# Maxima of q as a row of the transposed q from unit 2 on, and the last two tiles of a unit projected as 64-row pairs, in a fused attention and maxout kernel

## The chip, the cores and the metric

The kernel runs on one core of a Trainium2 chip. The core has five engines with instruction streams of their own: TensorE (PE: matmuls, with the weight load PEld beside it), VectorE (DVE), ScalarE (ACT), GpSimd (POOL) and SyncE (SP, which here only issues transfers). They share an on-chip memory (SBUF) and eight PSUM banks, into which PE writes its products. The metric is the time of one execution on the device in microseconds; lower is better. Three executions of the kernel before took 292.72, 292.85 and 293.96 us; the median is 292.85.

## The reference

Two stages that follow each other. The first is attention in linear form with a feature map, the second a feed-forward layer whose three hidden projections are joined by a maximum:

```python
def phi(x):                                    # x: 8 batches, 8 heads, 576 rows, 64 columns
    proj = np.einsum('bhsd,df->bhsf', x, w_phi)                      # 64 -> 128
    proj = proj - np.max(np.abs(proj), axis=-1, keepdims=True)
    return np.concatenate([np.exp(proj), np.exp(-proj)], axis=-1)
q_p, k_p = (phi(q), phi(k))
kv = np.einsum('bhsf,bhsd->bhfd', k_p, v)
z = np.sum(k_p, axis=2)
num = np.einsum('bhsf,bhfd->bhsd', q_p, kv)
den = np.einsum('bhsf,bhf->bhs', q_p, z)[..., None] + 1e-06
attn = num / den
x = attn.transpose(0, 2, 1, 3).reshape(8 * 576, 512)
h = np.maximum(np.maximum(x @ w1, x @ w2), x @ w3)                   # 512 -> 768
out = h @ w_out                                                      # 768 -> 512
```

All inputs and the output are float32. The row maximum of |proj| is what the change is about: for q it is subtracted from proj before the exponents are taken.

## The kernel before

**Units.** The 64 pairs of batch and head are handled four at a time: 16 units, each with 18 tiles of 128 rows (two pairs of heads, 8 full tiles each, and tiles 8 and 17, which hold the last 64 rows of each head). The tiles of a unit are worked in five groups, L37: four groups of four tiles and one of two, `(8, 2)`, the two last tiles.

**One unit, step by step.** q and k come in. For units 0 to 3 (BY_PE) POOL's queue loads them and turns float32 into bf16 on the way, and PE transposes them (L491), after which DVE copies them into qkT (L494). From unit 4 on SP loads them as float32, POOL casts them (L477), and SP transposes them by DMA (L506). SP loads v. In qkT, rows 0 to 63 hold the transposed q, rows 64 to 127 the transposed k.

- Projections G: for a group of four tiles PE makes a pair of 64-row products for each tile, q into the bank psq and k into the bank psk (L533). For the group of two tiles it makes one full product of 128 rows and 256 columns for each tile, and q and k lie side by side in the bank psq (L528).
- DVE takes the maxima of |proj| from these banks (L552): of q into mqp, of k into mk. ACT takes the two exponents of k into Ek (L546).
- From mk ACT makes the factors em (L584), and POOL multiplies v by them into vab (L588; units 0 and 1 in halves of nine tiles, one of them by DVE), and em itself is copied beside it (L598).
- Maxima of q, first form (`by_product`, units 0 to 3, since SUBT is 4): PE makes q's projection again, now transposed, into the bank psm (L615), and then for each tile of the group adds a product of the maxima with a negative identity (L618): 18 such products in a unit.
- Maxima of q, second form (units 4 to 15): PE transposes the maxima into the bank pmT (L560, the node R), ACT or DVE copies them to mT (L564), and a DMA writes mT as row 64 of qkT (L568, the node V), over k's first row. From units 4 on SP issues it; ACT issues it for units below V_ACT, which is 4, so so far for none. Then one matmul for a group, with a weight matrix wphi_m whose row 64 is -1 (L613), gives the projection less the maximum. Since the row replaces k's data, V waits for all of the unit's projections.
- ACT takes the two exponents of q from psm into Eq (L626).
- K: 72 products of Ek and vab (L642), copied to kv (L647). N: 40 products of Eq and kv (L660), divided on DVE (L666, L667) into x_sb. For units 0 to 5 PE transposes x_sb (L680), for the others a DMA does (L690), into xT.

**The second stage** runs in chunks of 512 tokens, one for each batch as soon as both of its units are through, and a last one for the 64-row tails of all batches: hidden products (L713), maxima (L719, L721, L723), output products (L741, L746), copies (L754) and stores (L761, by SP). The weights w1, w2, w3 and w_out are loaded by POOL's queue (L421). The maximum of three is taken as x@w1 + max(0, x@(w2-w1), x@(w3-w1)): POOL or DVE subtracts w1 from the two others in place (L788), and the straight part x@w1@w_out is a product (L741) with pm = w1@w_out, which PE makes once (L814) from w1 as it has turned it (L800).

**The order.** Nothing is scheduled at run time. Each step is a node with a number, a kind, costs, dependencies and buffers. The table PLAN, L97 to L243, lists all nodes in order; a word such as `64T10@11.8` says: node 64 on PE (T; D is DVE, A ACT, G POOL, S SP), buffer slots 1 and 0, planned start 11.8. The function plan (L250) reads it, and each engine executes its instructions in the order of the table. The table also fixes which of the eight banks each product gets, and two engines may not read one bank at the same time (locks): they follow one another. A change in the number of nodes or banks needs a new table.

**Fillers.** The function fill (L268) looks at the planned gaps on PE up to 28 us (WARM) and some after, and puts products into them whose result nobody reads (L846, into the bank of the buffer spare).

The queues: SP's loads, stores and transposes are hardware queues; POOL's loads with a change of type (q and k of units 0 to 3, w1, w2, w3, w_out) are a software queue, on which POOL's own engine is busy while it issues (L421 and the q, k loads some 0.7 to 0.9 us each). ACT issues one store at the end (281.41 us).

Of the kernel before, what the change touches and what calls it, by code (L numbers as in the profile page):

```python
# [16 lines left out]
DF = 128  # L17
DM = H * D
DFF = 768
P = 128  # L20
# [22 lines left out]
SUBT = 4  # L43
# [3 lines left out]
JOIN = 2  # L47
MOVE = 5
# [49 lines left out]
2D0@0.5 8S0@0.7 10S@1.3 4S@1.9 0G@0.5 6G0@1.1 7G@1.9 12S0@3.1 3D@0.8 9D@4.5 5D@5.5 11D@6.2 1G@2.8 1051G@3.2 13T1@5.9  # L98
14D0@6.7 82G1@4.0 83G@4.9 17T2@7.5 15T3@7.6 24T004500@8.0 19T67@8.4 18D@7.8 16D@8.3 22D@8.9 27D@9.5 29T12@9.1 39T3@9.3
34T64@10.3 32D@10.1 42D@10.7 37D@11.1 26A@8.6 25A@9.3 31A@9.7 21A@10.2 36A@10.9 35A@11.5 20A@12.0 33D@11.7 38D@12.3  # L100
43D@12.9 28D@13.2 23D@13.8 64T10@11.8 58T6@12.2 65A@12.5 66A@13.0 156G2@5.7 155G@6.6 1061T4@13.0 61T1@13.6 1065T0@14.1
55T5@14.7 52T7@15.2 41A@13.4 60A@13.7 48A0@14.2 62A@14.4 44A@14.9 59A@15.2 40A@15.7 53A@16.0 30A@16.5 57A@17.0
47A0@17.5 63A@17.6 56A@18.1 54A@18.6 49G@14.6 45G@15.7 1054G@16.8 1062D0@14.4 46G@17.6 51G@18.7 50G@19.0 1052G@20.1
84D1@15.6 1066D@15.7 86T4@16.4 90T6@16.9 88T3@17.1 87D1@17.2 89D@17.8 91D@18.4 92T110211@18.0 102T41@18.6 97T35@18.8
112T6@19.1 95D@18.6 96D@19.3 107T70@19.4 103A@19.1 113A@19.6 93A@20.0 108A@20.5 109A@21.1 85S@15.8 105D@19.9 110D@20.5
67T047@21.2 115D@21.1 100D@21.4 106D@22.0 94A@21.6 98A@22.1 104A@22.8 68A@23.3 128T31@22.3 1063T2@22.8 222G0@20.9
159T1@23.4 131T4@24.0 129A@23.7 116D@22.6 69D@23.0 111D@23.3 121A1@24.2 114A@24.4 123G1@24.6 124G@25.7 101D@24.0
137T7@24.6 130A@24.7 139A@25.2 117A@25.6 99A@25.8 138A@26.3 118G@26.0 119G@27.1 122G@28.2 125T0@24.8 132A@26.6
133A@27.3 120A@27.8 134T6@25.3 136A@27.9 135A@28.6 126A@29.0 127A@29.7 223G@29.3 76T30@25.8 1053G@30.2 1057G@31.0
1055G@33.1 1064D@24.6 160D2@25.7 74T2@26.1 70T5@26.5 77D0@26.3 71D1@27.0 75D0@27.6 1071T1@26.8 157D2@28.3 1072D@28.4  # L110
158S@28.5 165T00735400@28.1 161T2@28.7 163T1@29.2 169D@29.0 164D@29.6 168D@29.8 172D@30.4 162D@31.0 166A@30.2
167A@30.8 1073T6@29.3 140T110@30.7 173D@31.6 174T7532@31.9 182D@32.6 1074A@31.3 141A@32.1 181D@33.2 177D@33.8
183T6@32.3 142A@32.5 185A@32.9 180A@33.3 179A@34.0 1069T1@32.7 170A@34.5 1070A@35.0 72T0@34.0 149T31@34.3 178D@34.4
187D@35.0 186D@35.5 188A0@35.5 175A@35.7 191A0@36.2 1067T7@34.6 190G@35.9 189G@38.0 1068A@36.4 1056G@40.1 150D1@35.8
143T2@35.9 80T1@36.2 147T3@36.6 145T7@37.0 144D0@36.5 224D3@37.1 73D1@37.2 146D0@37.8 148D1@38.4 225S@37.3 356S1@38.0
355S0@38.6 359G1@43.2 358G@44.7 201T20@37.4 176A@36.9 184A@37.4 195T5@37.8 192T6@38.3 171A@37.7 81D@39.0 202A@38.2
203A@38.8 290S0@40.3 151T0@38.8 78T4@39.1 153T7@39.4 152D@39.5 1060D@40.2 154D@40.8 79D@41.3 204T3@39.7 226T2@40.0
207T010@40.5 193A@39.3 205A@40.2 206A@40.7 197A@41.0 228T3@41.6 230T7@42.2 227D0@41.7 194A@41.5 196A@42.0 208A@42.5
198T4@42.3 209D@42.3 229D@42.7 232T11625011@42.9 1097T1@43.5 1085T3@44.4 199A@43.1 234A@43.7 231D@43.3 239D@43.7
236D@44.4 212T70@45.3 235D@45.0 233A@45.1 289S1@42.9 293G2@46.7 292G@49.1 1086A1@45.6 200A@46.1 213D0@45.9 360S1@46.0  # L120
1098D@46.5 237A@46.6 1081T5@45.6 250T6@46.5 241T2374@46.7 253D@47.1 244D@47.6 1058D@48.2 248D@48.8 1082A@47.1
247A@47.6 243A@48.1 252A@48.6 238A@48.9 1079T1@47.3 1080A@49.4 251A@49.9 1077T5@48.3 1083T2@49.1 242A@50.2 1078A@50.7
421S0@50.6 1084A@51.2 1089T7@50.0 249D@49.4 254D@50.4 240D@50.7 1090D@51.4 245D@52.0 1059D@52.6 265T11@50.9 262T6@51.4
271T5@51.8 273A@52.3 246A@52.7 272A@53.2 210T0@52.1 214T2@52.4 211D1@53.2 215D0@53.8 1087T7@52.7 1093T3@53.6
216T4@54.5 548S1@51.2 294S2@52.5 422S0@57.8 547S1@58.4 357S0@59.7 266A@53.5 263A@54.0 267A@54.5 268T5@54.8 218T0@55.3
255A1@55.0 264A@55.2 219A@55.8 1099T2@55.6 259T1@56.4 258A1@56.5 257G@55.4 256G@57.5 269A@56.6 260A@57.2 261A@57.8
270A@58.3 1094D@54.7 217D1@55.3 1088D@56.0 1100D@56.7 291S1@61.2 1397G@59.5 361T00364000@56.9 368D@57.7 364D@58.4
1095T7@57.5 1091T2@58.5 1096D@59.0 1092D@59.6 369D@60.2 370T1453@59.3 362A@58.8 375A@60.2 1101T7@59.9 367A@61.0
363A@61.5 379T2@60.9 378D@60.8 377D@61.4 382D@62.0 373D@62.4 381A@62.5 376A@62.9 365D@63.0 383D@63.6 374D@63.9
1102T@61.1 1105T5@62.4 1106T@63.3 384T1@64.6 1103A0@63.3 380A@64.1 274T136@64.6 1107D1@64.8 387A0@64.7 385A0@64.9  # L130
424G0@59.9 366A@65.2 390A0@65.7 550G1@66.5 425G@67.6 295T11721511@66.0 300A@66.7 297A@67.2 388G@68.7 389G@70.8
386S@65.3 275D@66.0 298D@66.7 276D@67.3 281T01@66.5 1109T3@67.0 296A@67.9 372A@68.4 301A@68.9 371A@69.3 283T7@67.9
279T6@68.2 282D0@67.7 284D1@68.4 280D0@69.1 1110T@68.5 1111A2@70.1 299D@69.7 1113T0@69.8 302D@70.3 303D@70.9
304T7642@70.7 305A@71.5 277T3@71.3 307D@71.5 278D1@72.1 311D@72.7 426S0@68.9 484S0@71.8 394T10@71.7 423S2@72.4
396A@72.2 395A@72.8 1114T@71.9 313T5@73.2 1115A3@73.5 220T7@73.4 287T3@73.7 611S0@73.7 610S1@75.2 486S3@76.6 317D@73.7
221D@74.0 308D@74.5 285T1@74.0 286A@74.6 310A@75.3 306A@75.7 288D@75.1 406T040@74.4 391T7@75.5 403T1@75.8 404A@76.2
309A@76.6 405A@77.1 407D@75.7 408D@76.1 312D@77.2 316D@77.8 1125T3@75.9 397T4@76.8 1119T6@77.0 1131T0@77.9 1120D0@78.2
399A@77.4 398A@78.0 392A@78.5 393A@79.2 315A@79.6 318T1@78.8 1132D@79.0 319D1@79.6 321A1@80.0 314A@80.2 324G1@80.4
320S@80.0 551G@80.7 1104S@80.7 411T20@78.8 487G2@81.8 1126A@80.6 1117T4@79.1 1129T6@80.0 1127T0@80.9 400T7@81.8
1118A@81.1 1128A@82.0 322G@82.9 323G@85.0 402A@82.5 401A@83.1 1130D@81.7 412D0@82.3 1139T1@82.0 1140D@83.1  # L140
436T00534600@82.8 1121T0@83.4 442A@83.7 441A@84.3 437A@84.8 438A@85.4 439D@83.7 443D@84.3 444D@84.9 427T2715@84.5
434D@85.5 440D@86.2 430D@86.8 433A@85.9 1122A@86.4 1123T4@85.1 1137T6@86.0 445T1@86.9 325T31@87.1 447A@87.4 326A@87.7
1124A@88.2 1135T0@87.4 1145T2@88.2 327A@88.7 448D@87.9 1138D@88.2 449D@88.8 446A@89.3 450T4@89.1 1133T6@89.2
1136D@89.2 451D0@89.8 331T3@90.0 328T1@90.2 432A@89.7 428A@90.2 429A@90.8 330A@91.3 435D@90.3 1134D@90.9 340T104@90.5
332A@91.8 341A@92.3 342D@91.9 431D@92.2 1149T5@91.6 1150T@92.6 1151D0@94.1 329A@92.7 453A0@93.1 333A@93.4 334T6@93.9
613G0@87.1 335A@94.3 336A@95.0 552S1@82.2 485S1@85.1 553T11407111@94.1 571T3@94.7 614G@88.2 575D@95.2 557D@95.6
560D@96.2 1146T@95.0 454G0@93.5 488G@95.6 574D@96.8 674S0@89.5 675S0@90.1 559A@95.5 558A@96.1 555A@96.6 556D@97.1
561D@97.7 572A@97.3 1108S@90.7 1116S@91.9 337T5@96.3 1141T6@96.4 1152S@94.9 549S1@96.1 1142T@97.3 1147A1@97.6
1143D3@98.8 452S@96.7 562T7421@98.6 573A@98.2 554A@98.6 563A@99.4 339A@99.9 564A@100.2 338A@100.7 569D@99.4 570D@100.1
565D@100.7 1153T3@99.1 1154T@100.1 1155A0@101.7 566D@101.3 576T0@101.4 568A@102.3 567A@102.9 577D1@101.9 415T6@101.5  # L150
413T2@101.8 416D1@102.1 409T5@102.1 347T71@102.4 414D0@102.7 348D1@103.3 1148S@98.4 862S0@99.6 578S@102.2 673S1@102.9
457T40@102.8 469T0@103.0 677G1@96.8 456G@97.9 455G@98.2 459A@103.4 471A@103.9 470A@104.4 349T3@103.1 343T6@103.4
350D0@103.9 344D1@104.6 410D0@105.2 472T021@103.7 466T7@104.9 345T3@105.2 346D1@105.8 460T0@105.5 458A@104.7
579A1@105.2 468A@105.5 467A@106.1 419T6@105.7 417T4@106.0 463T5@106.4 420D@106.4 473D@106.9 461A@106.6 474A@107.1
418D@107.3 489S2@103.5 351T3@106.6 589T71@106.9 353T6@107.1 352D@107.7 354D@108.2 586T2@107.4 592T1@107.6 481T40@107.9
# [137 lines left out]
def kernel(  # L293
# [134 lines left out]
    def attention(u):  # L428
# [51 lines left out]
        tr = {}  # L480
# [37 lines left out]
        for part in joined:  # L518
            given, mms = [], []
            for t0, n in part:  # L520
                psq, psk = bank("psq", [P, 4, DF]), bank("psk", [P, 4, DF]) if n == 4 else None
                given.append((t0, n, psq, psk))

                def proj(t0=t0, n=n, psq=psq, psk=psk):
# [353 lines left out]
```

## Time and profile before

| what | us |
|---|---|
| median of three executions (292.72 to 293.96) | 292.85 |
| the profiled execution | 292.35 |
| its span, first to last instruction | 290.6 |
| PE at L713, hidden products, x411 | 100.7 |
| PE at L746 and L741, output products, x305 | 74.8 |
| PE at L642, x1152 | 20.5 |
| PE at L533, pairs of projections, x256 recorded | 20.4 |
| DVE at L552, maxima of q and k | 47.7 and 42.5 |
| ACT at L546 and L626, exponents | 70.5 and 79.2 |
| POOL at L588, vab | 68.2 |

The granted TensorE clock was 1.000. Busy times are the sums over the instructions of a line; those of PE overlap one another, since its matmuls are pipelined and each record reaches into the next, so the sum over its lines is more than its busy time. In a stream a product advances by less than its recorded mean. The chain that ended last spends 86% of the span on PE, 6% on DVE, 4% on ACT and 2% on DMA.

### The profile page before, as it was taken

Reading aid. Unit: us, or ns where it says so; the run is one execution under the profiler, and the core shown is the slowest. Engines: PE = TensorE matmul, PEld = TensorE weight load, DVE = VectorE, ACT = ScalarE, POOL = GpSimd, SP = SyncE. Lnnn points to the kernel's source line nnn. Section 1 sums busy time; section 2 is a strip of 40 time slices with the busy share of each in tenths; the row PEclk is TensorE's granted clock in tenths of the full one; section 3 lists DMA queues with packets and bytes.
Section 4 is the critical chain, followed back from the end, with each engine's and each line's share of the span. In section 5 each row is a group of like instructions: output and inputs, shape, how many; then the busy total and the mean of one; then the engine's idle time right before and its main releaser. Section 6 shows DMA issues by size and latency. Waiting matters only on the chain.

```text
span 290.6 us, 8659 instructions
## 1 busy us (share of the span) xinstructions
PE 279.4 (96%) x3602; PEld 158.7 (55%) x3641; DVE 215.9 (74%) x457; ACT 189.9 (65%) x438; POOL 117.4 (40%) x101
## 2 busy tenths in 40 slices
PE   8878999999999999999999999999999999999993
PEld 3556685646645585564466556545555564444442
DVE  2987999998876899768989959898796583242360
ACT  1599798977988899799669797566858631120101
POOL 8086886276093751552780519107064300000000
PEclk9999999999999999999999999999999999999999
DMA  7999988997967799796995779658534523500605
GB/s 191 208 201 181 218 249 271 230 335 178 356 132 258 221 189 279 165 287 130 298 182 106 173 235 206 138 126 174 102 107 95 112 21 72 126 18 2 144 18 128
DMA packets 63051, 49.87 MB, mean 172 GB/s; under 512 B 43556, under 2 KB 48036, under 8 KB 63012
## 3 DMA queue, kind: packets, MB, share of 16 engines
q1 hardware_dynamic: 58644, 44.04, 61.2%
q0 software_dynamic: 4288, 5.21, 11.0%
q8 instruction: 28, 0.46, 0.6%
q14 instruction: 11, 0.09, 0.1%
q10 hardware_dynamic: 80, 0.07, 0.1%
HBM read 34.67 MB, written 9.44 MB: 152 GB/s over the span
## 4 chain that ended last, share of the span: by engine, by line
PE 86%; DVE 6%; ACT 4%; DMA 2%; issue 1%; SPq 0%; ACTq 0%
PE ups L713 30%; PE ops L746 16%; PE ops L741 11%; PE kvps L642 7%; PE psn L660 6%; PE psq L533 5%; PE psm L613 4%; DVE mqp L552 2%; DMA wphi_f<-in_w_phi_dram 2%; DVE mk L552 2%; ACT Ek L546 2%; PE tps L491 1%; PE pxT L680 1%; PE psm L618 1%; PE psq L528 1%
## 5 line engine op out<-in xcount | busy, mean ns | idle before, releaser
L588 POOL TENSOR_TENSOR vab<-v_raw,em 128x1152 bf16<-128x1152 f32 (+1 forms) x36 | 68.2, 1907 | 88.7 <-ACT em L584 67.7
L713 PE MATMUL ups<-xT,w_bf 128*128 128x512 bf16 x411 | 100.7, 379 | 1.1
L546 ACT ACTIVATE Ek<-psk 128x512 bf16<-128x512 f32 x128 | 70.5, 607 | 23.7 <-PE psk L533 17.0
L626 ACT ACTIVATE Eq<-psm 128x512 bf16<-128x512 f32 (+1 forms) x160 | 79.2, 586 | 7.9 <-PE psm L613 6.2
L713 PEld LDWEIGHTS <-w_bf 128*128 128x128 bf16 x432 | 40.3, 98 | 44.1 <-DVE x_sb L667 0.2
L746 PE MATMUL ops<-wout_bf,hT 128*128 128x512 bf16 (+1 forms) x219 | 50.7, 373 | 0.3
L552 DVE TENSOR_REDUCE mqp<-psq 128x4 bf16<-128x512 f32 (+1 forms) x80 | 47.7, 631 | 2.0 <-PE psk L533 1.0
L719 DVE TENSOR_TENSOR hT<-hT,ups 128x512 bf16<-128x512 bf16 x54 | 35.9, 683 | 14.2 <-ACT hT L721 6.8
L552 DVE TENSOR_REDUCE mk<-psk 128x4 f32<-128x512 f32 x64 | 42.5, 681 | 1.7 <-ACT Ek L546 1.2
L746 PEld LDWEIGHTS <-hT 128*128 128x128 bf16 x222 | 21.3, 98 | 22.8 <-DVE hT L719 0.2
L721 ACT ACTIVATE hT<-ups 128x512 bf16<-128x512 f32 x28 | 16.4, 613 | 26.2 <-PE ups L713 26.1
L667 DVE TENSOR_TENSOR x_sb<-psn,rden 128x320 bf16<-128x320 f32 x64 | 31.5, 492 | 2.2
L660 PEld LDWEIGHTS <-Eq 128*128 128x128 bf16 x640 | 24.5, 97 | 6.5 <-issue 0.3
L754 DVE COPY osb<-ops 128x512 f32<-128x512 f32 (+1 forms) x19 | 12.6, 674 | 18.9 <-PE ops L746 18.9
L660 PE MATMUL psn<-kv_sb,Eq 128*128 128x65 bf16 x640 | 26.3, 193 | 0.1
L723 DVE TENSOR_SCALAR hT<-ups 128x512 bf16<-128x512 f32 x26 | 17.5, 686 | 11.4 <-PE ups L713 11.1
L754 ACT COPY osb<-ops 128x512 f32<-128x512 f32 (+1 forms) x18 | 10.3, 575 | 23.7 <-DMA out_dram<-osb 9.6
L741 PE MATMUL ops<-xT 128*128 128x512 bf16 x86 | 24.1, 380 | 0.5
L642 PEld LDWEIGHTS <-Ek 64*128 64x128 bf16 x1152 | 18.4, 94 | 5.7 <-issue 2.8
L642 PE MATMUL kvps<-vab,Ek 64*128 64x65 bf16 x1152 | 20.5, 190 | 0.9 <-POOL vab L588 0.5
L533 PE MATMUL psq<-w,qkT 64*128 64x128 bf16 x256 | 20.4, 217 | 0.4 <-DVE qkT L494 0.4
L533 PEld LDWEIGHTS <-qkT 64*128 64x128 bf16 x512 | 14.5, 94 | 10.7 <-issue 7.7
(72 smaller groups left out, 277.8 us busy)
## 6 DMA issues: line engine op xcount, KB each, us to landing
v_raw<-in_v_dram SPq DMA_DIRECT2D x16, 576.0 KB, 4.6
out_dram<-osb SPq DMA_DIRECT2D x70, 128.0 KB, 2.4
k_raw<-in_k_dram SPq DMA_DIRECT2D x12, 576.0 KB, 4.9
q_raw<-in_q_dram SPq DMA_DIRECT2D x12, 576.0 KB, 6.1
w_bf<-in_moe_w_dram POOLq DMA_DIRECT2D x3, 768.0 KB, 10.0
qk_bf<-in_q_dram POOLq DMA_DIRECT2D x3, 288.0 KB, 10.6
qk_bf<-in_k_dram POOLq DMA_DIRECT2D x3, 288.0 KB, 11.1
wout_bf<-in_moe_w_out_dram POOLq DMA_DIRECT2D x1, 768.0 KB, 9.5
```

What stands on the lines that cost most here:

```text
L533: nc.tensor.matmul(ps()[:, i, :], lhsT=cols[r, :], rhs=w2[r, c, :], start=True, stop=True)
L546: nc.scalar.activation(Ek[s]()[:, tiles_of(t0, n), :], of(1), EXP, scale=1.0 - 2.0 * s)
L552: nc.vector.tensor_reduce((mq, mk)[c]()[:, tiles_of(t0, n)], of(c), AXX, ALU.max, apply_absolute_value=True)
L588: (nc.vector if n_.eng == "DVE" else nc.gpsimd).tensor_tensor(vab()[:, g, t0:t1, 0:D], vb()[:, t0:t1, :], em()[:, g, t0:t1].unsqueeze(2).t ...
L626: nc.scalar.activation(Eqb()[s][:, cols], psm()[:, 0:w], EXP, scale=1.0 - 2.0 * s)
L642: nc.tensor.matmul(kvps[ab]()[:, t // NT, g, :], lhsT=Ek[g]()[r, t, :], rhs=vab()[r, g, t, :], start=(t + g == 0), stop=(t == UT - 1 and g ...
L660: nc.tensor.matmul(psn()[:, c, :], lhsT=Eqb()[g][:, t0:t0 + P], rhs=kv()[:, pr, ab, g, :], start=(g == 0), stop=(g == 1))
L667: nc.vector.tensor_tensor(x_sb()[:, pr, :, ab, :], psn()[:, :, 0:D], rden().to_broadcast([P, 5, D]), ALU.mult)
L713: nc.tensor.matmul(ups(), lhsT=w_bf[i + 1][:, ct, j * P:(j + 1) * P], rhs=tokens_of(ct), start=(ct == 0), stop=(ct == CT - 1))
L719: nc.vector.tensor_tensor(hT()[:, j, :], hT()[:, j, :], ups(), ALU.max)
L741: nc.tensor.matmul(ops_()[:, 0:width], lhsT=tile_of(ct, tt), rhs=line_w[c_i > MOVE][:, ct, cols], start=(ct == 0), stop=False)
L746: nc.tensor.matmul(ops_()[:, 0:width], lhsT=hT()[:, j, tt * P:(tt + 1) * P], rhs=wout_bf[:, j, cols], start=False, stop=(j == JT - 1))
```

## The change

Four things change at once.

1. SUBT goes from 4 to 2: units 2 and 3 take the second form for the maxima of q (R, mT, V and one matmul for a group in place of the products with the negative identity). V of these two units is issued by ACT, since V_ACT stays 4; no unit of the kernel before went that way.
2. TWO_BANKS = 2: from unit 2 on the two last tiles of a unit are projected like the others, as pairs of 64-row products, q into psq and k into a bank psk of its own. Units 0 and 1 keep the full products and the single bank. The maxima and exponents of these two tiles keep their shapes; they now read from two banks.
3. The table PLAN is new throughout: its 147 lines are replaced by 148, with other node numbers (units 2 and 3 have three nodes more), other banks and another order on every engine.
4. By the gaps of the new table fill makes 27 fillers instead of 23; 16 of them instead of 13 stand ahead of the first transpose.

What the new order moves at the start, as it stands in the instruction streams. POOL before: identity, q of unit 0 in two halves, the negative identity, w1's load (768 KB), q of unit 1, k of units 1 and 2, q of unit 2, two half vab of unit 0, the load of w_out, a half vab, a copy, a half vab, the second weight load, and so on, with the differences of weights (L788) further on. POOL after: q of unit 0, the identity, the negative identity, w1's load, q and k of unit 1, q of unit 2, the load of w_out, three half vab and two copies and a half vab, then k of unit 2, the second weight load, and further on a difference of weights between the copies of unit 1's em and the last three halves of its vab. SP sends one of k's two first halves, w_phi twice, k's second half and then three v; before both halves of k, w_phi and four v. One of k's first casts goes from DVE to ACT.

The diff, with the table cut (below the table the lines of the changed kernel stand 2 further down):

```diff
-SUBT = 4
+SUBT=2
...
 JOIN = 2
+TWO_BANKS = 2
...
 PLAN = """
-2D0@0.5 8S0@0.7 10S@1.3 4S@1.9 0G@0.5 6G0@1.1 7G@1.9 12S0@3.1 3D@0.8 9D@4.5 5D@5.5 11D@6.2 1G@2.8 1051G@3.2 13T1@5.9
...
-1444S@288.8
...
+1442S@285.5 1438S@287.3 1450S@288.5
 """
...
             for t0, n in part:
-                psq, psk = bank("psq", [P, 4, DF]), bank("psk", [P, 4, DF]) if n == 4 else None
+                psq, psk = bank("psq", [P, 4, DF]), bank("psk", [P, 4, DF]) if n == 4 or u >= TWO_BANKS else None
...
-                        if n == 2:
+                        if psk is None:
                             nc.tensor.matmul(psq()[:, 2 * i:2 * i + 2, :].rearrange("p a f -> p (a f)"), lhsT=cols,
                                              rhs=w2.rearrange("p a f -> p (a f)"), start=True, stop=True)
                             continue
...
-            a = nd("G", {"PE": 0.22 if n == 2 else 0.236 * len(part)}, lambda mms=mms: [f() for f in mms], [tr[ti], n_phi],
-                   [qkT, mk, mq] + tiles + Ek, mode=int(n == 4))
+            a = nd("G", {"PE": 0.22 if psk is None else 0.13 if n == 2 else 0.236 * len(part)}, lambda mms=mms: [f() for f in mms], [tr[ti], n_phi],
+                   [qkT, mk, mq] + tiles + Ek, mode=int(psk is not None))
...
-                    return (psq, psk)[c]() if n == 4 else psq().rearrange("p (t c) f -> p t c f", c=2)[:, :, c, :]
+                    return (psq, psk)[c]()[:, 0:n, :] if psk else psq().rearrange("p (t c) f -> p t c f", c=2)[:, :, c, :]
```

## The prediction

> **What bounds the kernel now.** I read the page's busy times first, then the stretches, then the chain of waits, then the rows of the instructions that the change touches.
>
> ```profile
> PE 279.4 (96%) x3602; PEld 158.7 (55%) x3641; DVE 215.9 (74%) x457; ACT 189.9 (65%) x438; POOL 117.4 (40%) x101
> ...
> 7.00:30.00 23.00, 19.65 (x393) 13.22 (x389) 19.72 (x43) 19.46 (x51) 12.15 (x14) 1.00 1.11 198
> 30.00:60.00 30.00, 29.68 (x524) 19.71 (x527) 28.10 (x61) 25.70 (x59) 20.41 (x13) 1.00 0.97 239
> 60.00:237.00 177.00, 175.41 (x2437) 100.49 (x2465) 145.30 (x307) 136.75 (x315) 78.30 (x61) 1.00 0.75 186
> ```
>
> The columns of a stretch are its length, then the busy time of PE, PEld, DVE, ACT and POOL, the granted clock, the DMA share and GB/s. From 30 us on PE is busy 205.1 of 207 us at a granted clock of 1.00: there its own work sets the end, and each microsecond of it that goes is a microsecond won, as long as the work can still be fed. Between 30 and 60 us that isn't sure, since DVE is busy 28.1 of 30. Before 30 us PE is not the bound: it stands idle for 3.4 of 23 us, and ten of its products are fillers (L846).
>
> **PE work that goes.** The chain of waits shows what a step costs when PE streams (start, length, what):
>
> ```profile
> 23.25 0.23 PE psm L618 x8
> 25.16 0.11 PE psm L618 x2
> 29.49 0.16 PE psq L533
> 29.65 0.05 PE psq L533
> ...
> 41.72 1.20 PE kvps L642 x72
> ...
> 61.78 0.22 PE psq L528 x2
> ...
> 65.45 0.06 PE pmT L560
> ```
>
> Units 2 and 3 lose the L618 products: four groups of eight (0.23 each) and one of two (0.11), 1.03 us a unit, 2.06 us. The wide matmul before them stays as long (L615 381 ns, L613 380 ns), so it counts nothing. Added: one transpose of the maxima a unit, 2 x 0.06 = 0.12.
>
> The last two tiles: 0.22 us for two full matmuls goes; two 64-row pairs come. A q/k pair of L533 advances 0.05 us in a stream, so 0.11 for both. 14 units x 0.11 = 1.54 us. Their DVE and ACT instructions keep their shapes; the second bank for k only lets them run side by side.
>
> Against it stands the step from full to 64-row matmuls: the first L533 takes 0.16 instead of 0.05, so 0.11 a change. The Trainium skill, page "TensorEngine Tiling (Array Packing)", section Key Properties, says that a change of tiling mode drains TensorE; the 0.16 agrees. If every new pair stood alone between full matmuls, 14 x 2 x 0.11 = 3.1 us would turn the 1.54 into a loss of 1.5. The order of PE's instructions decides: it has 97 changes of mode before and 99 after, so 0.2 us is my term.
>
> Sum: -2.06 + 0.12 - 1.54 + 0.2 = -3.3 us of PE work, all of it behind 24 us.
>
> **What the new order adds at the start.** Here PE waits, so the longest way through other engines counts.
>
> ```profile
> 1.04 5.73 PE L846 MATMUL idler<-idle 128*128 128x512 bf16 x13 [1.04 <-DVE idle L414]
> 6.70 0.80 PE L491 MATMUL tps<-ident,qk_bf 128*64 128x128 bf16 x16
> 15.53 2.26 POOL L588 TENSOR_TENSOR vab<-v_raw,em 128x576 bf16<-128x576 f32 x2 [8.62 <-ACT em L584]
> 21.00 0.83 POOL L421 DMA_DIRECT2D w_bf<-in_moe_w_dram  x1
> ...
> w_bf<-in_moe_w_dram POOLq DMA_DIRECT2D x3, 768.0 KB, 10.0
> ...
> L588 POOL TENSOR_TENSOR vab<-v_raw,em 128x1152 bf16<-128x1152 f32 x28 | 59.1, 2123 | 77.7 <-ACT em L584 56.8 <-issue 10.0 <-PE psk L533 8.8
> L788 POOL TENSOR_TENSOR w_bf<-w_bf 128x1024 bf16<-128x1024 bf16 x3 | 6.8, 2270 | 0.1
> ```
>
> The new order holds 16 fillers ahead of the first transpose, the old one 13. At 5.73/13 = 0.44 us each the first transpose moves from 6.70 to 8.0. I carry this 1.3 us to the first vab product: 15.53 becomes 16.85. On POOL the old order has two half vab, the wout load, two more with a copy, then the second weight load at 21.00. The new one has wout at the start, then four halves (1.13 each), two copies (0.27), the k load of unit 2 (0.71) and the weight load: 16.85 + 5.77 = 22.6, 1.6 us later. It lands after 10.0: 32.6. What is new is that POOL waits for it in the middle of unit 1: behind it stand a difference (2.27), three halves of unit 1's vab (3.39), a difference (2.27), unit 2's vab (2 x 2.12) and its copy (0.35). So unit 2's K, which the chain shows at 41.72, starts at 45.1: +3.4. Lower bound: with wout out of its way the load lands as early as the trace's shortest of this size (9.5), and back to back the POOL products start 0.05 to 0.2 apart less than their means, 44.1: +2.4. I take +2.9. Up to that K the orders give PE the same work within 0.3 us (20 transposes more, 26 small products fewer), so the 3.3 us lies behind it, and 0.25 more.
>
> **New waits.** Each row of maxima (4.5 KB) now goes out on ACT's queue: the issue holds ACT some 0.56 us (as its only DMA does at 281.41), and unit 2's copy of it 0.25; 1.4 us in all, hidden while ACT has 4.3 idle us of the 30 between 30 and 60. Behind the issue wait a copy of pm and exponents of k; without cover it costs those 1.4. The matmuls L613 of units 2 and 3 now wait for it to land, besides for unit 2's and 3's last projections. I lay out 3.7 and 3.3 us of PE work between issue and first reader. The landing isn't recorded; bounds: its packets are through 1.6 us after the issue when the queue is empty (219.95), and the shortest distance to a reader is 4.06 us (195.36 to 199.43). Cost 0 to 0.8 a unit; I take 0.1 each, nearest to the empty queue, as ACT's holds nothing else. The page "DMA: Bandwidth & Descriptors" of the Trainium skill, section Queues, rings and completion order, says that each DMA engine goes round the queues that have work; by that the row doesn't stand behind SP's six loads and the term is nothing. No run here shows it. The k load of unit 2 goes out at 21.9 instead of 5.5: it lands 4.7 (a half-sized one at the start) to 10.6 us later, and its transposes come at 28 to 29, so 0 to 3.5 us of wait, of which the late K of unit 2 hides most; 0.2. In all +0.4, bounds 0 to 3.
>
> **The sum.** -3.3 - 0.25 + 2.9 + 0.4 = -0.25 us. The profiled execution took 292.35 us (span 290.6 and 1.75 around it), the median is 292.85; so 292.1 on its scale, 292.6 on the median's. Half a per cent (1.46 us: 291.39 to 294.31) is about what a measurement can tell from no change.
>
> **Rivals.**
> 1. The maxima come late (slower). SP sends six 576 KB loads just while unit 2's row of maxima goes out. If the row shares their delay (they land in 4.6 to 6.1 us), it decides from 3.3 us on: 5.0 us after the issue costs 1.3 and 1.7 us in PE's order, +2.8 over my term: 295.4. For: PE reads the row in order, and no other work stands behind it. Against: another queue, 4.5 KB.
> 2. The loads collide (slower). Those six loads used to go out from 38.5 us, when POOL's transfers were through; now they go from about 33 us, over the q and k of unit 3 on POOL's queue. The k load of 29.41 took 8.0 us beside one such load, against 1.45 us between landings in a full queue; two or three beside it would make unit 3's transposes (about 42.5) 2 us late: 294.6.
> 3. The delay at the start doesn't carry (faster). Then K of unit 2 comes at 43 instead of 44.6, since the fillers only fill time in which q, k and w_phi land (the chain has w_phi at 7.86): -1.85: 291.0.
> 4. The pairs don't pay: q and k of the last tiles run one after the other, and 1.5 us stays: 294.1. Against: psq and psk of L533 overlap in every group.
>
> **Numbers.** Forecast 0.50 (own range 291.3 to 293.9, of which 0.06 faster, 0.04 slower), rival 1 0.13, rival 2 0.13, rival 3 0.19 (0.14 of it beyond half a per cent), rival 4 0.05. Faster 0.06 + 0.14 = 0.20; slower 0.04 + 0.13 + 0.08 of rival 2 + 0.01 of rival 4 = 0.26; same 0.54. Range 290.9 to 295.0: below it about 0.07, above it 0.11, mostly rival 1.
>
> **What will show it.** PE's busy time without fillers falls by about 3.3: the groups of L618 (L620 in the changed kernel, whose lines below the table stand 2 further down) and L528 (L530) shrink to 68 and 4 instructions, and those two alone change in count besides L533 and L560. K of unit 2 stands at 44 to 45 us; POOL's first L790 (the old L788) waits for w_bf. If K stands at 42 and the end is at 289, rival 3. If PE waits at the L615 of units 2 and 3 (the old L613), rival 1; at the transposes of unit 3, rival 2. I'm wrong altogether if the stretch from 60 us on, where only pairs change, differs by more than 2 us from the 1.3 that I give it.

## The result, and the profile after

The changed kernel is slower: 295.81 us (median of 16 executions, 294.37 to 297.40) beside 294.00 us for the kernel before on the same chips (16 executions, 291.55 to 296.36; the 292.85 above was the median of the first three). The ratio is 1.0087, with a 95% interval of 1.0059 to 1.0115. The profiled execution took 297.40 us, of which 295.6 are its span. All ratios leave out executions that are disturbed, over 1.5% above the fastest of their kernel, here four of the kernel before; with these four the two medians give 1.0062.

The first line is from the page of the changed kernel (busy time, share and count of instructions for each engine), the others are its stretches, with the columns of the prediction's first fence:

```profile
PE 280.8 (95%) x3607; PEld 156.8 (53%) x3607; DVE 214.1 (72%) x458; ACT 190.3 (64%) x434; POOL 117.7 (40%) x106
...
7.00:30.00 23.00, 20.40 (x416) 14.11 (x417) 20.20 (x43) 19.63 (x49) 10.54 (x16) 1.00 1.10 203
30.00:60.00 30.00, 27.10 (x422) 16.85 (x421) 25.88 (x58) 21.86 (x51) 22.03 (x16) 0.94 0.95 236
60.00:237.00 177.00, 174.25 (x2448) 97.72 (x2447) 143.14 (x302) 136.46 (x316) 78.89 (x62) 1.00 0.78 186
```

Between 30 and 60 us PE is busy 27.10 of 30 us where it was 29.68, and the granted clock, 1.00 before, is 0.94. The chain of waits of the changed kernel says what it stood for (start, length, what):

```profile
34.45 6.37 DMA qkT<-mT
40.82 0.04 issue
40.86 0.72 PE psm L615 x3
41.58 1.44 PE psn L662 x30
...
46.57 1.25 PE kvps L644 x72
```

Waits of PE in the same execution from 30 to 60 us (total, times, longest):

```profile
PE psm L615 <- DMA qkT<-mT: 2.6, 1, 2.6
```

ACT issues unit 2's row of maxima at 34.45; the first matmul that reads it runs at 40.86. PE had work until 38.3, so the 3.7 us of work that the prediction laid out between the two were there, and then stood for 2.57 us. K of unit 2 starts at 46.57, not at 41.72 as before. The stretches of the same kernel around that wait show a second loss behind it:

```profile
40.00:42.00 2.00, 1.14 (x18) 0.89 (x19) 0.04 (x1) 0.49 (x1) 1.95 (x1) 0.93 1.05 409
42.00:44.00 2.00, 2.00 (x27) 1.45 (x25) 1.33 (x4) 2.00 (x6) 2.00 (x2) 0.50 1.05 394
44.00:46.00 2.00, 2.00 (x49) 1.80 (x46) 1.47 (x5) 1.13 (x3) 2.00 (x4) 0.72 0.64 232
```

The clock column (third from the end) falls to 0.50 after the wait: 2 x (0.07 + 0.50 + 0.28) = 1.7 us of PE's clock are gone, in which PE looks busy. DMA (second from the end) is above 1, that is, all 16 engines are taken.

The POOL timeline of the changed kernel (start, length, line, what; in brackets the idle time before it and what ended it) tells of the start:

```profile
29.94 2.12 POOL L790 TENSOR_TENSOR w_bf<-w_bf 128x1024 bf16<-128x1024 bf16 x1 [0.46 <-DMA w_bf<-in_moe_w_dram]
32.03 3.37 POOL L590 TENSOR_TENSOR vab<-v_raw,em 128x576 bf16<-128x576 f32 x3
35.35 2.12 POOL L790 TENSOR_TENSOR w_bf<-w_bf 128x1024 bf16<-128x1024 bf16 x1
40.05 4.20 POOL L590 TENSOR_TENSOR vab<-v_raw,em 128x1152 bf16<-128x1152 f32 x2 [2.58 <-DMA v_raw<-in_v_dram]
```

The wait for the second weight is there, but 0.46 us long and over at 29.94, not at 32.6. What POOL stands for is another load, unit 2's v: issued at 31.61, waited for until 40.05.

The groups of the removed work are as foretold (line, engine, what, count, busy time and mean ns):

```profile
L620 PE MATMUL psm<-minus,mqp 128*128 128x64 bf16 (+1 forms) x68 | 3.6, 194 | 0.1
...
L562 PE MATMUL pmT<-ident,mqp 128*128 128x128 bf16 x14 | 3.1, 221 | 0.1
...
L530 PE MATMUL psq<-w,qkT 128*128 128x256 bf16 x4 | 0.8, 274 | 0.1
```

Two measures are used below, both taken from the traces. The first is the row's way: from the issue of unit 2's row to its first and last packet. The second is PE's lost time up to a moment: the time gone, less the sum of the steps that a stream takes for each product started by then (0.216 us for 512 columns, 0.109 for 256, 0.056 for a pair of 64-row products, for q's and k's transposes of a tile together or for another transpose, 0.029 for L618 and 0.056 for its products of 128 columns, 0.030 for L660, 0.0155 for L642; a product whose record is missing is counted by its weight load); fillers, waits, a slow clock and changes of mode count as lost. Without what is lost, the work of PE by these steps is 260.3 us in the kernel before, 256.8 in the changed one (3.5 less), and 258.7 where units 2 and 3 keep the old products (no_row, spread_no_row).

### The profile page after: what moved, and what is told of

Its sections match the earlier page's. It is cut to its first block, busy times and chain, and to the rows that moved or that the text cites. A ratio compares the mean times of both kernels' runs of the same rounds, so it can differ in the third digit from the quotient of the medians.

```text
span 295.6 us, 8643 instructions
## 1 busy us (share of the span) xinstructions
PE 280.8 (95%) x3607; PEld 156.8 (53%) x3607; DVE 214.1 (72%) x458; ACT 190.3 (64%) x434; POOL 117.7 (40%) x106
## 4 chain that ended last, share of the span: by engine, by line
PE 82%; DMA 7%; ACT 5%; DVE 3%; POOL 1%; issue 1%; ACTq 0%; DVEq 0%; POOLq 0%
PE ups L715 31%; PE ops L748 15%; PE ops L743 11%; PE psn L662 6%; PE kvps L644 6%; PE psm L615 5%; PE psq L535 4%; DMA qk_bf<-in_k_dram 4%; DMA qkT<-mT 3%; ACT Ek L548 3%; ACT Eq L628 2%; PE pxT L682 1%; DVE hT L721 1%; PE tps L493 1%; POOL qk_bf L462 1%
## 5 line engine op out<-in xcount | busy, mean ns | idle before, releaser
L548 ACT ACTIVATE Ek<-psk 128x512 bf16<-128x512 f32 (+1 forms) x156 | 79.1, 572 | 21.3 <-PE psk L535 14.0
L628 ACT ACTIVATE Eq<-psm 128x512 bf16<-128x512 f32 (+1 forms) x160 | 77.2, 580 | 14.0 <-PE psm L615 13.5
L554 DVE TENSOR_REDUCE mk<-psk 128x4 f32<-128x512 f32 (+1 forms) x78 | 47.6, 633 | 1.9 <-PE psk L535 1.6
L721 DVE TENSOR_TENSOR hT<-hT,ups 128x512 bf16<-128x512 bf16 x54 | 35.5, 681 | 12.8 <-PE ups L715 11.6
L756 ACT COPY osb<-ops 128x512 f32<-128x512 f32 (+1 forms) x22 | 12.7, 583 | 33.6 <-PE ops L748 31.9
L748 PEld LDWEIGHTS <-hT 128*128 128x128 bf16 x222 | 20.9, 98 | 22.6
L723 ACT ACTIVATE hT<-ups 128x512 bf16<-128x512 f32 x27 | 16.0, 606 | 22.2 <-PE ups L715 22.1
L662 PE MATMUL psn<-kv_sb,Eq 128*128 128x65 bf16 x640 | 27.4, 196 | 0.6 <-DVE kv_sb L649 0.6
L615 PE MATMUL psm<-qkT,wphi_m 128*128 128x512 bf16 (+1 forms) x70 | 20.6, 366 | 4.2 <-DMA qkT<-mT 4.2
L535 PE MATMUL psk<-w,qkT 64*128 64x128 bf16 x284 | 22.7, 217 | 0.9 <-issue 0.9
L535 PEld LDWEIGHTS <-qkT 64*128 64x128 bf16 x568 | 16.3, 94 | 13.0 <-issue 10.8
L756 DVE COPY osb<-ops 128x512 f32<-128x512 f32 (+1 forms) x15 | 9.9, 668 | 17.6 <-PE ops L748 13.4
L535 PE MATMUL psq<-w,qkT 64*128 64x128 bf16 x284 | 22.7, 217 | 0.0
## 6 DMA issues: line engine op xcount, KB each, us to landing
wout_bf<-in_moe_w_out_dram POOLq DMA_DIRECT2D x1, 768.0 KB, 17.2
```

The costliest lines, as they stand in the source:

```text
L535: nc.tensor.matmul(ps()[:, i, :], lhsT=cols[r, :], rhs=w2[r, c, :], start=True, stop=True)
L548: nc.scalar.activation(Ek[s]()[:, tiles_of(t0, n), :], of(1), EXP, scale=1.0 - 2.0 * s)
L554: nc.vector.tensor_reduce((mq, mk)[c]()[:, tiles_of(t0, n)], of(c), AXX, ALU.max, apply_absolute_value=True)
L615: nc.tensor.matmul(psm()[:, 0:w], lhsT=wphi_m, rhs=rhs, start=True, stop=True)
L628: nc.scalar.activation(Eqb()[s][:, cols], psm()[:, 0:w], EXP, scale=1.0 - 2.0 * s)
L662: nc.tensor.matmul(psn()[:, c, :], lhsT=Eqb()[g][:, t0:t0 + P], rhs=kv()[:, pr, ab, g, :], start=(g == 0), stop=(g == 1))
```

## The experiments

All ratios are to the kernel before, in executions on the same chip. The table lists those with their intervals, and what their traces show of unit 2: the row's way (first and last packet after its issue), PE's wait at the first matmul that reads the row, the start of unit 2's K, and PE's lost time at 38 and 60 us and at the end.

| run | ratio, 95% interval | row, us | wait | K of unit 2 | lost at 38, 60, end |
|---|---|---|---|---|---|
| before, first profile | 1 | none | none | 41.7 | 16.5, 17.8, 30.3 |
| before_again | one execution | none | none | 41.6 | 16.5, 19.9, 32.5 |
| changed kernel | 1.0087 (1.0059 to 1.0115) | 4.4, 5.7 | 2.57 | 46.5 | 17.2, 22.5, 38.8 |
| again | 1.0066 (1.0034 to 1.0098) | 4.3, 5.7 | 2.58 | 46.6 | 17.2, 22.5, 37.8 |
| row_first | 1.0102 (1.0045 to 1.0159) | 6.1, 6.5 | 3.31 | 47.9 | 17.1, 24.0, 38.6 |
| loads_later | 1.0196 (1.0144 to 1.0248) | 4.2, 4.4 | 1.24 | 50.2 | 17.2, 26.3, 40.6 |
| no_row | 1.0079 (1.0037 to 1.0120) | none | none | 44.8 | 18.6, 21.7, 35.5 |
| v_early | 1.0092 (1.0054 to 1.0129) | 4.3, 4.9 | 2.07 | 44.5 | 17.1, 21.6, 36.9 |
| rows_ahead (the profiled execution took 299.73 us) | 1.0101 (1.0033 to 1.0170) | 2.9, 3.6 | none | 44.2 | 18.3, 23.5, 41.1 |
| both | 1.0126 (1.0067 to 1.0185) | 3.3, 4.4 | 0.99 | 45.3 | 17.1, 21.2, 36.8 |
| full_rows | 1.0121 (1.0065 to 1.0177) | 4.3, 5.0 | 1.74 | 44.6 | other products |
| calm | 1.0106 (1.0054 to 1.0158) | 3.1, 4.3 | 1.00 | 43.2 | 17.1, 22.1, 38.7 |
| calm_all | 1.0068 (1.0036 to 1.0099) | 3.1, 4.5 | 1.51 | 44.4 | 17.4, 21.4, 37.0 |
| spread | 1.0056 (1.0019 to 1.0093) | 1.5, 1.7 | none | 43.0 | 17.7, 23.5, 38.0 |
| w3_later | 1.0114 (1.0058 to 1.0169) | 4.1, 5.7 | 2.47 | 46.8 | 17.4, 25.1, 41.2 |
| spread_full | 1.0079 (1.0047 to 1.0111) | 1.5, 1.6 | none | 43.1 | other products |
| spread_no_row | 1.0056 (1.0019 to 1.0094) | none | none | 43.0 | 16.7, 20.1, 34.3 |

One point of the code matters for the edits. What the prediction's front calls the order of the table is, in the end, the order of the planned starts: `fill` sorts all nodes by them before they are issued. Where an edit gives a word another start, its instruction moves on its engine. In the diffs below, the words of both and w3_later stand without those that they replace (in loads_later 427S0@32.8 becomes 427S@32.8), and the runs whose row is a word of SP (190S) have row_first's change of on_act too.

**again: the same kernel once more.**

> The changed kernel once more, unaltered, for a second profile. Theory A (the row of maxima of unit 2 stands behind the loads that SP has just sent): PE waits 2 to 3 us at the first L615 of unit 2, 38 to 41 us into the span, and the granted clock falls below 1.00 in the 5 us after it. Theory B (the loss is a mishap of the one profiled execution and the steady loss lies elsewhere, for example at unit 8's row, which SP sent 6 us after its maxima were transposed): no wait above 1 us at unit 2. Ratio to before 1.006 to 1.012 by both.

Theory A's picture came back to a hundredth. Waits of PE between 30 and 60 us in this run (total, times, longest):

```profile
PE psm L615 <- DMA qkT<-mT: 2.6, 1, 2.6
```

The clock fell again (0.84, 0.50 and 0.80 in the same three stretches). The other suspect is there too: at unit 8's row PE waits 0.74 us (1.66 in the first profile). So the wait is steady; whether it is what the change costs, the next runs were to tell.

**row_first and loads_later: two edits that did something else than meant.**

```diff
 row_first
-            on_act = u < V_ACT
+            on_act = u < V_ACT and u != 2
-190A@35.3
+190S@35.3
 loads_later
+    late = nodes[427].bufs[0]
+    node("gate", 6, {"DVE": 0.1}, lambda: nc.vector.memset(late()[0:1, 0, 0:1], 0.0), [], [late])
+1456D0@36.9
```

> The row of unit 2 is issued by SP, ahead of five of the six loads (the five go out 2 to 3 us later). Theory A: the row lands within 3 us of its issue, PE doesn't wait for it, the clock stays at 1.00, and 2.6 us of wait and some 1.7 us of slow clock go: ratio to before 0.993 to 0.998. Theory A2 (POOL's software loads, which run until 38 us, hold the row, not SP's): it lands 5 to 6 us after its issue, ratio 1.007 to 1.011. Theory B: ratio as the changed kernel, 1.0087, though PE doesn't wait at unit 2.

> The row stays on ACT's queue; five of the six loads are held until DVE has finished the maxima of unit 2 (about 36.5 us instead of 32.0 to 34.2), by a small DVE write into their first buffer. Theory A: the row lands within 3 us, no wait at unit 2, ratio 0.993 to 0.999 (the later loads may cost up to 1 us at unit 5's casts). Theory A2 (POOL's loads or ACT's own queue make it slow): the wait of 2 to 3 us stays, ratio 1.007 to 1.011.

Because of the sort by planned start, in row_first the first two of the five loads (planned at 32.8 and 33.4) still stood ahead of the row on SP. Its first packet came 6.1 us after the issue, later than on ACT's queue. In loads_later the small DVE write, planned at 36.9, came behind the first load instead of ahead of it, and DVE waited 4.3 us for that load to land: the ratio 1.0196 is the price of that, and says nothing of the loads. What row_first shows is that a row behind three loads of 576 KB in the same queue (unit 2's v and these two) was worse off than one beside six in another.

**no_row: units 2 and 3 by the old products in the new order (six words go, and the numbers behind them move up).**

```diff
-SUBT=2
+SUBT=4
-188T0@34.4 189A0@34.9 190A@35.3
-258T1@49.3 259D1@49.6 260A@50.7
```

> Units 2 and 3 take the products with the negative identity again (68 more small products, no transpose of the maxima, no copy, no row), in the otherwise unchanged new order. The row's way can't be waited for. Theory A: 4.3 us of wait and slow clock go, 1.9 us of PE work come back: 2.4 us less than the changed kernel, ratio 0.999 to 1.002. Theory B: no wait to win, PE work added: ratio 1.012 to 1.016.

1.0079: neither. The wait for the row is gone and K of unit 2 starts at 44.8, 1.7 us sooner, for 1.9 us more work of PE. Within this K the chain of waits has something else:

```profile
44.84 0.86 PE kvps L643 x50
45.71 1.66 issue
47.37 0.54 PE kvps L643 x22
```

In the middle of its 72 products PE stands 1.66 us and waits for no semaphore ("issue"); there is such a wait of 1.19 us at 26.1 too. Theory A falls in its simple form: with the row gone, another wait takes its place a few us behind.

**v_early, rows_ahead, both: the two late things, alone and together.**

```diff
 v_early
-157D2@31.9 158S@32.2
+157D2@27.4 158S@27.5
 rows_ahead
-190A@35.3 427S0@32.8 362S1@33.4 361S1@35.3
+190S@35.3 427S0@35.41 362S1@35.42 361S1@35.43
 both
+157D2@27.4 158S@27.5 190S@35.3 362S1@35.41 361S1@35.42 228S@35.43 427S0@35.44 428S0@37.7
```

> Unit 2's v (the load that POOL waited for until 40.05 us in the changed kernel, 2.6 us) goes out about 4 us earlier: the small DVE write that holds it back stands ahead of the copies of unit 2's transposes instead of behind them. Nothing else moves; the row of maxima stays on ACT's queue behind six loads. Theory C (two ways of equal length, the row and the v, each sent beside the same loads; either one alone makes unit 2 late): POOL's wait falls below 1 us, PE's wait of 2 to 3 us at unit 2's L615 stays, ratio 1.005 to 1.009. Theory D (the v alone sets unit 2's K, the row's wait is only where PE happens to stand): ratio 0.997 to 1.002.

> The row of unit 2 is issued by SP, this time ahead of all five loads that follow unit 2's v (in the earlier run with the row on SP, two of them still stood ahead of it). So unit 2's v has SP's queue to itself until the row is out, and five loads wait for the row's issue (about 35.2 us). Theory C: both ways get short, PE waits under 0.5 us at unit 2, the clock stays at 1.00, K of unit 2 starts at 43 to 44.5 us instead of 46.5, ratio 0.995 to 1.000. Rival (POOL's software loads, which run until 38 us, keep the 16 DMA engines full by themselves): the row lands 5 us after its issue as before, ratio 1.006 to 1.010.

> The earlier v and the row ahead of the five loads, and among these the loads of unit 5 and unit 3 ahead of those of unit 6, which are needed some 40 us later. Theory C: as the run with the row ahead, and up to 1 us less: ratio 0.992 to 0.998. Rival (POOL's loads fill the engines): 1.004 to 1.009.

In again unit 2's vab was ready at 44.4 and K started at 46.6, so v didn't set this K; but without the row K couldn't have started before 44.4. In v_early POOL's wait for v is gone (its vab starts at 36.96, not 40.05) and K of unit 2 comes 2 us sooner; the ratio stays. Most of the 2 us isn't POOL's: the wait for the row ended 0.7 us sooner (40.16 instead of 40.86), and behind it the clock stayed at 1.00 in this execution, which fits the other 1.3. In both, the row too comes sooner (wait 0.99), and the ratio stays. The DVE timeline of both shows where the time went:

```profile
36.91 1.95 DVE L790 TENSOR_TENSOR w_bf<-w_bf 128x1024 bf16<-128x1024 bf16 x1 [1.33 <-DMA w_bf<-in_moe_w_dram]
38.79 0.68 DVE L820 CAST xT<-pm 128x512 bf16<-128x512 f32 x1
39.39 2.00 DVE L790 TENSOR_TENSOR w_bf<-w_bf 128x1024 bf16<-128x1024 bf16 x1
41.31 0.42 DVE L649 CAST kv_sb<-kvps 128x260 bf16<-128x260 f32 x1
```

Two differences of the third weight take 1.95 and 2.00 us, and unit 1's kv copy, for which PE waits 1.69 us, stands behind them. Beside a POOL that stands still, such a difference takes 0.67. POOL's vab run from 36.20 to 38.31 and from 38.28 to 40.84: each difference ends 0.55 us after the vab beside it, as if it had waited for its end (again: POOL's operation to 37.02, the difference to 37.58). The Trainium skill, page "SBUF — State Buffer", section "SBUF: two separate sides", says that a DVE operation with two inputs in SBUF and a POOL operation that reads SBUF lock each other out for the whole instruction. The traces agree: all fifteen differences on DVE that took longer than 0.70 us began while an operation of POOL ran, and ended 0.54 to 0.56 us after it. So an earlier v puts POOL's vab beside DVE's differences, and gives the gain back there.

**full_rows: do the pairs pay?**

```diff
-                            r = slice(c * D, (c + 1) * D)
+                            r = slice(c * D, (c + 1) * D) if n == 4 else slice(0, P)
```

Here, and in spread_full below, the two products of each of the last two tiles read all 128 rows of the transposed q and k, so their q and k are others than the reference's.

> The last two tiles of units 2 to 15 go into two banks as in the changed kernel, but by products over all 128 rows (with the zero half of w2), one for q and one for k, instead of 64-row pairs that run side by side. This takes back only the work saved on PE: 14 units x 0.11 us, less the changes of mode. If the term of 1.5 us is right: ratio 1.005 above the changed kernel in the same runs, 1.011 to 1.015 to before. If the pairs save nothing that PE's path feels: within 0.002 of the changed kernel, 1.006 to 1.010.

1.0121, which is 0.0034 to 0.0055 above the changed kernel's two measurements (1.0087 and 1.0066), where 1.5 us of 294 are 0.0051. The size would fit a full gain by the pairs, but the intervals (some 0.005 to each side) overlap, and the medians of all executions (296.22 and 294.32) give 1.0065, no more than the changed kernel's. So this run doesn't show that the pairs pay.

**calm and calm_all: the differences moved away, and unit 8's row and unit 6's loads too.**

```diff
 calm (both, and)
-1066D@38.4 1065D@37.2
+1066D@49.75 1065D@50.3
 calm_all (calm, and)
-584S@103.3 427S0@35.44 428S0@37.7
+584S@102.95 427S0@49.0 428S0@49.1
-1154S@99.5 1158S@100.7
+1154S@103.05 1158S@103.06
```

> The run with the earlier v and the row ahead of the loads, and two of DVE's three differences of the third weight moved from 36.9 and 39.4 us to about 50 us, where POOL makes no vab. In the run without this move they took 1.95 and 2.00 us each beside POOL's vab (0.67 to 0.68 where POOL stands still), and PE waited 0.5 and 1.7 us for the DVE copies behind them. Theory E (the won time was lost again to DVE and POOL slowing each other): these two waits go, each difference takes 0.7 to 1.0 us, unit 2's K starts at 43 to 43.5 us, 1.5 to 2.2 us less than that run: ratio 1.000 to 1.006. Rival (another wait takes their place, since 24 to 44 us is bound by transfers): K of unit 2 stays at 45, ratio 1.008 to 1.013.

> As calm, and unit 8's row goes out ahead of four stores on SP (in the changed kernel it waited there until 109.51 us and PE waited 1.66 and 0.74 us for it in two profiles), and the q and k loads of unit 6 go out at 49 us instead of 36. Theory E with the row of unit 8: 0.5 to 1.5 us less than calm, ratio 0.996 to 1.002. If the transfers are the bound, the later loads of unit 6 shorten the wait for unit 5's q (1.5 us on POOL) as well; if not, POOL's wait stays and the ratio is calm's within 0.003.

The differences of calm (line, engine, what, shortest/median/longest ns):

```profile
L790 DVE TENSOR_TENSOR w_bf<-w_bf x3: 668/671/674, 51.2 to 52.4; 128x1024 bf16<-128x1024 bf16 x3
```

As theory E said they are back at 0.67 us, PE's waits for DVE at unit 2 are gone and K of unit 2 starts at 43.2. But the time isn't less: 1.6 us later PE stands 2.07 us for "issue", that is, for no semaphore at all. In calm_all that wait is missing and unit 8's row isn't waited for; its unit 6 is late instead (POOL waits 3.8 us for its k, and PE 0.9 for a K behind that): I had moved its loads too far.

**before_again: has the kernel before such waits?**

> The kernel before, unaltered, for a second profile of it: the first had a clock of 1.000 and 292.35 us, while most of its executions since lie at 292 to 296 us with clocks of 0.99 to 1.00. If it has waits on PE of its own that the first profile lacked, they show here; else PE waits for no DMA and its granted clock stays at 1.00 from 30 to 60 us.

It has. The chain of the kernel before in this execution (294.54 us):

```profile
41.64 1.20 PE kvps L642 x72
42.84 0.51 PE tps L491 x13
43.35 2.02 issue
```

After K of unit 2, among small products, PE stands 2.02 us. In the first profile (292.35 us) this wait wasn't there, and one of 0.91 us was at 26.1. So the first profile was a good execution, and this one, nearer to the median of 294.00, pays 2 us right behind the place where the changed kernel pays for its row. What it waits for can be read from the packets: a 16 KB packet of the instruction queue ended at 44.07, and PE went on at 45.37. The same in the first profile (25.59 and 27.02), calm (45.53 and 46.88), v_early (46.26 and 47.60), spread (45.22 and 46.60), the changed kernel at unit 9 (129.18 and 130.68) and again there (128.54 and 129.80): PE goes on 1.3 to 1.5 us after such a packet each time. In all seventeen traces together PE stands so for more than 0.5 us 24 times behind the start, and each time it goes on 1.2 to 1.7 us after the end of such a packet. That PE lacks instructions there is my reading of this pattern.

**spread, w3_later, spread_full, spread_no_row: is the stage bound by the transfers as a whole?**

```diff
 spread (calm, and)
-1059G@27.3 427S0@35.44 428S0@37.7 584S@103.3
+1059G@36.2 427S0@47.1 428S0@47.2 584S@102.95
-1154S@99.5 1158S@100.7
+1154S@103.05 1158S@103.06
 w3_later (the changed kernel, and)
+1059G@36.2 1066D@49.75 1065D@50.3
 spread_full (spread, and)
-                            r = slice(c * D, (c + 1) * D)
+                            r = slice(c * D, (c + 1) * D) if n == 4 else slice(0, P)
 spread_no_row (spread, and)
-SUBT=2
+SUBT=4
-188T0@34.4 189A0@34.9 190S@35.3
-258T1@49.3 259D1@49.6 260A@50.7
```

> As calm, with three transfers taken out of the stage or put ahead: the load of the third weight goes out at about 36 us instead of 27 (its differences stand at 50 us since calm), the q and k of unit 6 go out after those of unit 4 (about 45 us), and unit 8's row goes out ahead of four stores. Theory F (the transfers of 24 to 46 us as a whole are the bound): the row lands within 3.5 us of its issue, PE waits less than 0.7 us for it, no wait for instructions after unit 2's K, K of unit 2 at 42.5 to 43.5 us; ratio 0.996 to 1.002. Rival (not the transfers: the order of the engines' work itself is longer): the waits go, the time stays, ratio 1.005 to 1.010.

> The changed kernel with the load of the third weight at about 36 us instead of 27, and two of its differences at 50 us; the row stays on ACT's queue behind SP's loads, unit 2's v goes out as late as before. Theory F: row and v land 1 to 2 us sooner (768 KB fewer in front), PE waits 1 to 2 us at unit 2 instead of 2.6: ratio 1.002 to 1.007. Rival (only SP's six loads matter): the wait stays at 2.6, ratio 1.006 to 1.010.

> As spread, with the last two tiles by products over all 128 rows: 1.5 us of PE work more. If PE's work sets the time once the waits are gone: 0.005 above spread. If not: within 0.002 of it.

> As spread, with the products with the negative identity in units 2 and 3 instead of the rows: 1.9 us of PE work more and no row to wait for. If PE's work sets the time there: 0.004 to 0.007 above spread. If the rows cost in waiting what they save: within 0.002 of it.

The stretches in which the row goes out, of the changed kernel and then of spread (the DMA share is second from the end):

```profile
34.00:36.00 2.00, 2.00 (x11) 0.94 (x11) 2.00 (x5) 0.60 (x3) 2.00 (x3) 1.00 1.17 241
36.00:38.00 2.00, 2.00 (x79) 1.41 (x78) 2.00 (x3) 1.89 (x7) 1.47 (x1) 1.00 1.11 331
...
34.00:36.00 2.00, 1.86 (x14) 0.87 (x12) 1.96 (x5) 1.60 (x5) 2.00 (x2) 1.00 0.17 33
36.00:38.00 2.00, 1.95 (x61) 1.22 (x62) 1.56 (x3) 1.13 (x5) 1.96 (x3) 1.00 0.39 25
```

In spread the row's way is what it is in an empty queue, 1.5 to 1.7 us, and K of unit 2 starts at 43.0. In w3_later, where POOL's load is out of the way but SP's six stay ahead, it is as slow as ever (DMA share 1.03 from 34 to 38 us), and the ratio, 1.0114, is no better. So both sets of transfers hold the row up, each by itself: 3.1 to 3.3 us to the first packet beside POOL's alone (both, calm; unit 2's early v is in that queue too), 4.1 beside SP's (w3_later), 4.3 to 4.4 beside the two. That part of theory F is shown. The other part isn't: spread is at 1.0056 (1.0019 to 1.0093), where theory F gave 0.996 to 1.002. Its chain of waits:

```profile
43.07 1.20 PE kvps L644 x72
...
44.60 2.00 issue
46.60 0.21 PE psk L535
```

It meets the same wait after K as the kernel before, followed this time by a clock of 0.84, 0.50 and 0.80 from 46 to 52 us. And its lost time grows by 2.3 us from 48 to 60 us (21.2 to 23.5), through this and what I moved there, where it grows by 0.4 in before_again (19.5 to 19.9).

The last two runs weigh the parts in this order. Without the rows of units 2 and 3 the ratio is the same, 1.0056, though PE then has 1.9 us more work: what these rows save, their order loses again, to within the intervals (some 1.1 us to each side). With products of 128 rows for the last two tiles it is 1.0079, 0.0023 more where 1.5 us make 0.005; the medians, 296.01 and 295.48 us, differ by 0.5, and the intervals overlap. Whether the pairs pay, anywhere from nothing to the whole 1.5 us, these runs don't show. No version here beats the kernel before.

## Why the prediction was wrong

The forecast was no change, 292.6 us or 0.25 us less than the median; measured is 0.87% more (0.59 to 1.15%), 2.5 us on that median. Rival 1, which had a chance of 0.13, gave 295.4, 2.55 us more, with the right place and the right mechanism up to a point. That its number fits is luck: it added two waits, 1.3 and 1.7 us at units 2 and 3, to a start 2.9 us late; the run has one wait of 2.57 us at unit 2 and none at unit 3, 1.7 us of slow clock, a start 0.7 us late and a loss from 60 us on that no rival held. And without the rows the time was as long (no_row, spread_no_row).

- **PE work that goes: right.** L620 and L530 have 68 and 4 products left, as named. By the sums of steps PE's work is 3.5 us less (260.3 and 256.8), as the terms said without the changes of mode. These are 97 and 99 in the traces as well, and a change between full and 64-row products costs 0.10 to 0.12 us in the median, so that term (0.2) held. PE's busy time, which was to fall by 3.3, doesn't show it (279.4 before, 280.8 after): it holds fillers and slow clock too.
- **The start: wrong in its way.** The term was +2.9 us, by the late second weight. The load went out at 20.55 (not 22.6), since POOL's halves began at 15.07 and not at 16.85, so the fillers didn't carry (the first transpose started at 6.95 us, not at 8.0); it landed by 29.94 and POOL waited 0.46 us. PE's lost time at 38 us is 0.7 us above that of before_again. Rival 3's condition held for the start; only what came behind it ate the gain. K of unit 2 did start late, at 46.5 against the 44 to 45 of the forecast, but behind the row's wait and the slow clock; without the row it came at 44.8.
- **New waits: the step that failed.** I took 0.1 us for unit 2's row, "nearest to the empty queue, as ACT's holds nothing else", with a bound of 0.8 from the shortest distance to a reader elsewhere. Neither fits this place: the row has a queue of its own and yet shares the 16 DMA engines with POOL's loads (until 38 us) and SP's six. It landed 5.7 us after its issue instead of 1.6, and PE waited 2.57. The page "DMA: Bandwidth & Descriptors" of the Trainium skill, section Queues, rings and completion order, has each DMA engine go round the queues that have work. The trace doesn't bear out that the term is nothing by that: the row's packets began 3.0 us later than in an empty queue (4.4 against 1.4 to 1.5). The distance of 4.06 us that I used as a bound came from a stretch in which the engines were far from full; the profile's stretches showed a DMA share of 0.97 from 30 to 60 us and 0.75 later, and I didn't use it. The same profile had a nearer bound: the rows issued at 96.89 and 137.10 us, each behind one load, took 3.2 and 2.9 us to their last packet, at DMA shares of 0.90 and 0.92. The issue itself held ACT for 1.32 us, not 0.56.
- **Not in the account at all: the clock.** The 2.57 us of wait drew 1.7 us of slow clock behind them. The price of a wait on PE has this second part.
- **Rival 2, the loads collide: half right.** Unit 3's transposes weren't late; unit 2's v was. POOL waited 2.58 us for it until 40.05 (in the kernel before 2.13 us, until 37.38), and its vab was ready 2 us before K started: hidden behind the row, and next in line.
- **The stretch from 60 us on: wrong.** I gave it 1.3 us less and said I'd be wrong altogether beyond 2 us from that. PE loses 15.3 us there in again and 12.6 in before_again, 2.7 more. Of these, 0.74 are unit 8's row, which SP sent 5 us after its maxima were transposed, behind a DMA transpose (6.7 us on SP) and four stores, and 0.8 a wait for no semaphore after two K in a row (at 126.2 and 127.3); both lie in the new order, not in the pairs. The rest, about 1.2, is spread over many steps and has no name; the changes of mode aren't it (68 there instead of 67).
- **The balance of a typical execution:** again lost 5.3 us more than before_again (0.7 until 38 us, 1.9 from there to 60, 2.7 behind) and had 3.5 less work: +1.8 us, as the two spans (294.6 and 292.8) say.

So the change took the work off PE that it was to take, and by this balance the new order lost that and more. Of the losses only the row's wait is traced to its cause by edits (spread, w3_later), and taking it away didn't bring the time back. Single remedies moved the wait to the next late thing (the row, v, DVE's differences beside POOL, PE's instructions), and seven reorderings (v_early, rows_ahead, both, calm, calm_all, spread, w3_later) lie between 1.0056 and 1.0126. That these four are all there are isn't shown.

## What to carry to other kernels

A queue of its own doesn't keep a transfer of a few KB fast while the DMA engines are full: lay out the work in front of its reader by the DMA share of that stretch and by what stands ahead in its queue, not by a calm stretch of the same kernel. Before costing a reordering, list everything that is due in the same few microseconds (rows, loads, operations that two engines can't do side by side, instructions), since removing one wait only shows the next. And a first profile may be a lucky execution: a second one of the kernel before showed 2 us of wait that the first lacked.

## What the runs showed of the hardware

- The clock falls after short waits, and goes by a grid. In every trace the granted clock changes only at multiples of 3.41 us, counted from where it first rises to 1.00, and a fall to 0.50 lasts 3.41 or 6.83 us, which costs 1.7 or 3.4 us of clock (1.7 in the changed kernel). From 24 to 285 us, each of the seven steps of this grid in which PE stood for 1.99 us or more at full clock was followed by half clock (1.99 to 2.81 us), and none in which it stood for 1.98 or less. So of four waits of 2.00 to 2.07 us only that of spread was followed by it: it lay within one step, those of before_again, v_early and calm across two. The Trainium skill, page "TensorE: Matmul & The Clock Gate", Part 1, names an idle window of about 3.4 us for it; here some 2 us within one step were enough, and the measurement decides.
- DVE's difference of two arrays in SBUF: 0.67 to 0.68 us by itself, up to 2.51 us when it began beside an operation of POOL, ending 0.54 to 0.56 us after that.
- PE stood 0.6 to 2.1 us, waiting for no semaphore, in dense stretches of small products (72 of K and what follows), and went on 1.2 to 1.7 us after a 16 KB packet of instructions, in all seventeen traces. The packets themselves took 0.9 to 1.4 us; what makes them late stays open.
